# Experts 1 to 6 sorted by token count on the chip and computed at six widths, and the underflow mask replaced by a flag

## The chip, the cores and the metric

The kernel runs on one core of a Trainium2 chip. TensorE (PE) multiplies, VectorE (DVE), ScalarE (ACT) and GpSimd (POOL) do elementwise work, and SyncE (SP) and the others issue transfers. Each engine has its own queue of instructions. The metric is the device time of one launch in microseconds (us), as the median of several runs; less is better.

## The reference

Attention with pooled queries gives x, 1152 tokens of 512 values. Each token chooses two of eight experts; expert e takes its own tokens through two matrices with a ReLU between. A last dense block multiplies by w_in, applies h*cos(h) and multiplies by w_out. These two matrices, 512x2048 and 2048x512, come as 64-bit floats.

```python
top2 = np.argpartition(-noisy_logits, 2, axis=1)[:, :2]
...
for e in range(E):
    for k in range(2):
        mask = top2[:, k] == e
        h = np.maximum(x[mask] @ w1[e], 0.0)
        out[mask] += top2_w[mask, k, None] * (h @ w2[e])
...
h = x @ w_in
g = h * np.cos(h)
return (g @ w_out).astype(np.float32)
```

With the drawn inputs the experts 0 to 7 get 293, 306, 271, 255, 298, 284, 290 and 307 tokens.

## The kernel before

The program is written out in the order in which each engine runs it; a wait is put in wherever an instruction needs another engine's or a transfer's result. It has three parts: attention (to about 290 us of the profile), the experts (304 to about 575), the dense block (from there to the end).

**Routing.** `route` finds for every token its two experts and a row of the DRAM buffer `xg_d` for each. `scatter` writes the tokens there: 18 indirect transfers, issued by POOL one after another, each behind a tiny memset of `SPACER`. Expert 0 does not wait for them: its input is gathered on PE (`hot`). Expert 1 is loaded back from `xg_d` by POOL (`x_load(1)`, L961), later experts by SP.

**Experts.** Every expert has CAP = 320 slots for tokens, used or not. The loop runs over e and f, eight steps f for each expert, with s = 8e + f. In a step PE does `h_mm` (L975: 12 matmuls with 320 moving columns, since 32-bit values are split in a high and a low part and three products are made), ACT writes the high part `hh` (L985), DVE the low part `hl` (L986), and one step later PE does `yt_mm` (L1006: 12 more matmuls of 320 columns, 8 with `hh`, then 4 with `hl`) into four accumulators. So an expert has 8 x 24 = 192 matmuls. The next expert's tokens are loaded (`x_load`, tile `xr`), transposed on PE in four groups (`x_tr`, L967) and split by ACT and DVE (`x_split`, L913, L914). For expert 1 this stands at the end of expert 0 (f = 7): two groups of transposes, `yt_mm(0, 7)`, two more groups.

**Weights.** A unit is half a megabyte of w1 or w2. SP loads it into one of three `raw` buffers, ACT (L558) and DVE (L559) split it into `u`; `advance_c` runs this some units ahead of PE. All these stand in one queue for each engine with the steps' other work.

**Decode.** DVE turns 64-bit weights into 32-bit ones in 16 chunks during the experts: `dec_load` (two transfers of 512 KB by SP), then `dec` in three steps, DVE L1055, L1059, L1063. Values too small for 32 bits must become zero: ACT takes the absolute value (L1061), POOL makes a 0/1 mask (L1062) and multiplies (L1065) before it stores the chunk (L1066).

**Overflow.** `counts_of` (end of step s = 2) counts tokens per expert with one matmul and two DVE reductions; at the very end each engine loads the largest count, and a general path runs if it is over 320.

## Time and profile before

| | us |
|---|---|
| median of 3 runs | 793.23 (790.15 to 795.38) |
| the profiled execution | 794.18 |
| its span, first to last instruction | 792.3 |
| PE busy in it | 762.4 (96%) |
| DVE, ACT, POOL busy | 616.8, 508.2, 396.0 |

The span leaves about 2 us of the execution's own time outside. Busy time of PE includes pipelined waiting, so idle gaps and the granted clock have to be read from the timeline.

### The profile page before, as it was taken

The numbers are of one execution on the slowest core, as the hardware profiler recorded it, in microseconds if no ns is written. First come the engines' busy times: TensorE is split into PE (matmuls) and PEld (weight loads), VectorE is DVE, ScalarE is ACT, GpSimd is POOL, SyncE is SP. The second block draws the span as 40 slices with busy tenths as digits, with TensorE's granted clock in tenths as the row PEclk, the third lists the DMA queues.
The fourth block names the chain that finished last, engine by engine and source line by source line (L and its number), as shares of the span: only waits on it lengthen the run. The fifth ranks groups of instructions, "written<-read, shape, count | busy, mean of one in ns | idle before, by whom it ended". The sixth has DMA issues, their size and how long they took to land.

```text
span 792.3 us, 14073 instructions
## 1 busy us (share of the span) xinstructions
PE 762.4 (96%) x4976; PEld 703.7 (89%) x4976; DVE 616.8 (78%) x1226; ACT 508.2 (64%) x1218; POOL 396.0 (50%) x364
## 2 busy tenths in 40 slices
PE   7799999999999999799999999999999999999996
PEld 4689989999999989799999999999888999889995
DVE  5478778877888897379999999878678687785663
ACT  5689789879979854355654545555467566565553
POOL 4868767867878848316556666575056120100000
PEclk9899999999999999989999999999998999999999
DMA  9829688796964206967979979796633210100001
GB/s 211 174 61 208 149 206 205 209 251 148 244 154 146 61 18 213 333 204 235 331 254 317 306 268 348 245 334 212 221 102 118 80 31 25 54 1 27 2 1 43
DMA packets 91164, 133.67 MB, mean 169 GB/s; under 512 B 27952, under 2 KB 58032, under 8 KB 91088
## 3 DMA queue, kind: packets, MB, share of 16 engines
q1 hardware_dynamic: 84688, 111.21, 49.7%
q0 software_dynamic: 5392, 18.48, 6.5%
q10 hardware_dynamic: 1008, 3.02, 1.5%
q8 instruction: 41, 0.67, 0.3%
q14 instruction: 35, 0.29, 0.1%
HBM read 81.24 MB, written 29.88 MB: 140 GB/s over the span
## 4 chain that ended last, share of the span: by engine, by line
PE 72%; DVE 11%; DMA 5%; ACT 4%; POOL 3%; issue 3%; SPq 1%; ACTq 0%; DVEq 0%; POOLq 0%
PE h L975 17%; PE acc L975 12%; PE acc L1006 9%; PE s L282 9%; PE pa L360 8%; PE pt L322 7%; PE t L975 3%; DMA kt<-st 3%; DVE u L559 1%; PE t L967 1%; PE t L1022 1%; POOL xg_d L525 1%; PE pt L608 1%; DMA xr<-xg_d 1%; ACT cr L1327 1%
## 5 line engine op out<-in xcount | busy, mean ns | idle before, releaser
L298 DVE TENSOR_REDUCE nm<-s 128x1 f32<-128x384 f32 x216 | 108.0, 550 | 35.8 <-PE s L282 21.6
L307 ACT ACTIVATE p<-s,nm 128x384 f32<-128x384 f32 x216 | 126.2, 593 | 1.4 <-DVE nm L300 0.5
L975 PE MATMUL h<-xe,u 128*128 128x320 f32 x768 | 125.9, 313 | 0.0
L975 PEld LDWEIGHTS h<-xe,u 128*128 128x128 f32 x768 | 114.1, 188 | 2.2
L1062 POOL TENSOR_SCALAR raw<-raw 128x1024 f32<-128x1024 f32 x16 | 65.7, 4107 | 95.0 <-ACT raw L1061 90.7
L559 DVE TENSOR_TENSOR u<-raw,u 128x1024 fp32r<-128x1024 f32 x66 | 88.9, 1351 | 18.9 <-ACT u L558 18.7
L322 PE MATMUL pt<-ident,p 128*128 128x128 f32 x645 | 95.1, 275 | 0.2 <-DVE X L633 0.2
L282 PE MATMUL s<-kt,q 128*128 128x384 f32 x240 | 84.2, 372 | 7.8 <-DMA kt<-st 4.1
L335 ACT ACTIVATE eh<-pt 128x384 fp32r<-128x384 f32 x144 | 63.1, 491 | 39.3 <-PE pt L322 37.3
L360 PE MATMUL pa<-eh,v 128*128 128x320 f32 (+1 forms) x279 | 87.1, 326 | 0.0
L360 PE MATMUL pa<-el,v 128*128 128x320 f32 (+1 forms) x279 | 82.9, 311 | 0.0
L322 PEld LDWEIGHTS pt<-ident,p 128*128 128x128 f32 x645 | 77.6, 142 | 5.5 <-issue 1.9
L558 ACT ACTIVATE u<-raw 128x1024 fp32r<-128x1024 f32 x73 | 76.6, 1054 | 7.6 <-DMA raw<-w_d 4.6
L339 DVE TENSOR_TENSOR el<-pt,eh 128x384 fp32r<-128x384 f32 x144 | 73.2, 549 | 4.0 <-ACT eh L335 2.3
L1006 PE MATMUL acc<-hh,u 128*128 128x320 f32 x448 | 76.3, 313 | 0.0
L346 POOL TENSOR_TENSOR el<-rw,eh 128x384 fp32r<-128x384 f32 x71 | 71.7, 1010 | 5.9
L1006 PEld LDWEIGHTS acc<-hh,u 128*128 128x128 f32 x448 | 68.5, 190 | 0.1
L975 PE MATMUL acc<-u,gh 128*128 128x512 f32 x216 | 68.2, 397 | 0.0
...
L345 POOL TENSOR_SCALAR eh<-rw 128x384 fp32r<-128x384 f32 x71 | 36.6, 515 | 53.3 <-ACT rw L343 45.5
L282 PEld LDWEIGHTS s<-kt,q 128*128 128x128 f32 x240 | 44.8, 192 | 16.4 <-ACT p L307 7.7
L282 PE MATMUL s<-kt,l 128*128 128x384 f32 x168 | 56.6, 337 | 0.0
...
## 6 DMA issues: line engine op xcount, KB each, us to landing
raw<-in_moe_w_dram SPq DMA_DIRECT2D x64, 512.0 KB, 5.9
raw<-in_moe_w_in_dram SPq DMA_DIRECT2D x16, 512.0 KB, 4.5
raw<-in_moe_w_out_dram SPq DMA_DIRECT2D x16, 512.0 KB, 6.7
w_d<-dw POOLq DMA_DIRECT2D x16, 512.0 KB, 6.5
raw<-w_d SPq DMA_DIRECT2D x14, 512.0 KB, 4.2
xg_d<-ZERO SPq DMA_DIRECT2D x10, 512.0 KB, 5.1
...
```

What stands on the lines that cost most here:

```text
L282: nc.tensor.matmul(o, l, r, start=(m == 0), stop=(not lo and m == len(mm) - 1))
L298: nc.vector.tensor_reduce(NM[n][:, i:i + 1], SB[n][i][:, 0:384], axis=AX.X, op=OP.max, negate=True)
L307: nc.scalar.activation(P[n][i], SB[n][i][:, 0:384], AF.Exp, bias=NM[n][:, 3:4], accum_out=SUMS[:, t, 2 * hp + hl, i:i + 1])
L322: nc.tensor.transpose(p[:, c], P[n][j][:, c], ident)
L339: nc.vector.tensor_tensor(el, t_src(n, j), ef, op=OP.subtract)
L346: nc.gpsimd.tensor_tensor(el, rw, ef, op=OP.subtract)
L360: nc.tensor.matmul(st["p"][:, 0:w], V2[hp, hl, b][:, c, :], (EH, EL)[s][:, c, EB[g]:EB[g] + w], start=(c == 0 and s == 0), stop=(c == 8 an ...
L558: nc.scalar.activation(b[:, 0], r, AF.Copy)
L559: st_w["lo"].tensor_tensor(b[:, 1], r, b.bitcast(F32)[:, 0], op=OP.subtract)
L975: nc.tensor.matmul(o, l, r, start=first and i == 0, stop=last and i == len(seq) - 1)
L1006: nc.tensor.matmul(ACC[e, d][:, 0:CAP], w[:, i, 128 * d:128 * d + 128], r, start=f == 0 and r is hh and i == 0, stop=f == 7 and r is hl)
L1062: nc.gpsimd.tensor_scalar(m, m, 2.0 ** -15, 0.0, op0=OP.is_ge, op1=OP.add)
```

## The change

CAPS gives a width to each place in the loop: 320 for place 0 and 7, which keep experts 0 and 7, and 282, 288, 294, 302, 312, 320 for places 1 to 6. `counts_of` moves from the end of step 2 to the end of step 0. It now multiplies the counts by 8, adds the expert's number, sorts the eight numbers with one DVE `max` and takes the low three bits as the experts' ids (`RANKI`); it also fills a small tile of limits, `LIM`, which lies in the tile `U0`, by nine memsets on POOL. At the end of step 1 `load_ids` loads six ids into registers of SP and one into a register of POOL. Loads of weights and tokens and stores of results for places 1 to 6 take their address from these registers.

The mask of the decode is gone from POOL. ACT instead sums up, chunk by chunk, how far values lie under the limit (`FL`); in the last block (`small_weights`, i = 52) one matmul spreads the flag, and the general path, which now applies the mask itself, runs if a flag or a limit was passed. The first chunk's decode starts one step later (s = 9), the first two `dec_load` move from steps 5 and 6 to 7 and 9, and `yt_mm(0, 7)` now stands ahead of all four groups of `x_tr(1, ...)`.

```diff
     make_identity(nc, ident)
     XROWS = NT * 8 * 128
     CAP = 320
+    CAPS = (CAP, 282, 288, 294, 302, 312, CAP, CAP)
+    TOP = float(N)
     xg_d = dram.tile([XROWS, DM], F32, name="xg_d")
     y_d = dram.tile([XROWS, DM], F32, name="y_d")
     FF2 = w_in.shape[1]
...
                 if next(g, 0) == 0:
                     gens.remove(g)
 
+    def small_weights():
+        m = CNT8[:, 1:2]
+        nc.vector.tensor_reduce(m, FL, axis=AX.X, op=OP.max)
+        nc.vector.tensor_scalar(FLB, m.to_broadcast([128, 2]), 0.0, None, op0=OP.is_gt)
+        p = tb2()
+        nc.tensor.matmul(p[:, 0:2], ONES, FLB, start=True, stop=True)
+        nc.vector.tensor_scalar(m, p[:, 0:1], TOP, TOP, op0=OP.mult, op1=OP.min)
+        nc.vector.tensor_tensor(CNT, CNT8[:, 0:1], m, op=OP.max)
+
     def mix_weights():
         nc.vector.tensor_scalar(ROWC, ROW, 3071, None, op0=OP.min)
         d = WT[:, :, 1]
...
         nc.vector.reciprocal(w, w)
         nc.vector.tensor_tensor(d, w, d, op=OP.mult)
 
+    LIM = U0.rearrange("p t e -> p (t e)")[:, 0:10]
+
     def counts_of(bank):
         p = bank()
+        for i in range(8):
+            nc.gpsimd.memset(LIM[:, i:i + 1], 8.0 * CAPS[6 - i] + 7.0 if i < 6 else 8.0 * E_N * N)
+        nc.gpsimd.memset(LIM[:, 8:10], 8.0 * CAP + 7.0)
         nc.tensor.matmul(p[:, 0:8 * NT], ONES, MK.rearrange("p t e -> p (t e)"), start=True, stop=True)
         nc.vector.tensor_reduce(CNT8, p[:, 0:8 * NT].rearrange("p (t e) -> p e t", e=8), axis=AX.X, op=OP.add)
-        nc.vector.tensor_reduce(CNT, CNT8, axis=AX.X, op=OP.max)
+        nc.vector.scalar_tensor_tensor(CNT8, CNT8, 8.0, IOTA8, op0=OP.mult, op1=OP.add)
+        nc.vector.tensor_tensor(LIM[:, 8:10], CNT8[:, 0:8:7], LIM[:, 8:10], op=OP.subtract)
+        nc.vector.memset(CNT8[:, 0:8:7], 0.0)
+        nc.vector.max(RANK, CNT8)
+        nc.vector.tensor_copy(RANKI, RANK)
+        nc.vector.tensor_scalar(RANKI, RANKI, 7, None, op0=OP.bitwise_and)
+
+    def over_of():
+        nc.vector.tensor_tensor(LIM[:, 0:8], RANK, LIM[:, 0:8], op=OP.subtract)
+        nc.vector.tensor_reduce(CNT8[:, 0:1], LIM, axis=AX.X, op=OP.max)
+        nc.vector.tensor_scalar(CNT8[:, 0:1], CNT8[:, 0:1], 0.0, TOP, op0=OP.max, op1=OP.min)
+
+    EID = {0: (0, 0), 7: (7, 7)}
+
+    def load_ids():
+        def one(c, eng):
+            return nc.values_load(RANKI[0:1, c:c + 1], engines=[eng], min_val=0, max_val=E_N - 1)
+        for i in range(1, 7):
+            EID[i] = [one(6 - i, mybir.EngineType.SP), None]
+        EID[1][1] = one(5, mybir.EngineType.Pool)
+
+    def rows_of(e, which, st, n):
+        r = EID[e][which]
+        if e in (0, 7):
+            return slice(st * 1024 + e * 128, st * 1024 + e * 128 + n)
+        return bass.ds(r * 128 + st * 1024, n)
+
+    ysts = []
+
+    def y_store(eng, e, st, n, src):
+        eng.nop()
+        d = eng.dma_start(y_d[rows_of(e, 0, st, n)], src)
+        for o in ysts:
+            tc.declare_no_dep(d.ins, o.ins, reason="each expert and each block has rows of its own")
+        ysts.append(d)
 
     scat = []
 
...
         if u < NCONV:
             e, i = divmod(u, 8)
             if i % 2 == 0:
-                src = w1[e].rearrange("(a p) f -> p a f", p=128)[:, :, 128 * i:128 * i + 256]
+                we = w1[e:e + 1] if e in (0, 7) else w1[bass.ds(EID[e][0], 1)]
+                src = we.rearrange("o (a p) f -> p (o a) f", p=128)[:, :, 128 * i:128 * i + 256]
                 nc.sync.dma_start(r.rearrange("p (a f) -> p a f", a=4), src)
             else:
-                src = w2[e].rearrange("(a p) d -> p a d", p=128)[:, i - 1:i + 1, :]
+                we = w2[e:e + 1] if e in (0, 7) else w2[bass.ds(EID[e][0], 1)]
+                src = we.rearrange("o (a p) d -> p (o a) d", p=128)[:, i - 1:i + 1, :]
                 nc.sync.dma_start(r.rearrange("p (a d) -> p a d", a=2), src)
         else:
             st_w["eng"].dma_start(r, w32_d[u - NCONV])
```

```diff
-        mm3(o[:, 0:CAP], [(w[:, 0, kd, c], w[:, 1, kd, c], xh[:, kd], xl[:, kd]) for kd in range(4)], True, True)
+        n = CAPS[e]
+        mm3(o[:, 0:n], [(w[:, 0, kd, c], w[:, 1, kd, c], xh[:, kd, 0:n], xl[:, kd, 0:n]) for kd in range(4)], True, True)
         late = e == E_N - 1 and f >= 4
         hh, hl = ((hxs[0] if late else me).tile([128, CAP], F32R, name=f"h{i}", bufs=4) for i in "hl")
-        nc.scalar.activation(hh, o[:, 0:CAP], AF.Relu)
-        nc.vector.scalar_tensor_tensor(hl, o[:, 0:CAP], 0.0, hh.bitcast(F32), op0=OP.max, op1=OP.subtract)
+        nc.scalar.activation(hh[:, 0:n], o[:, 0:n], AF.Relu)
+        nc.vector.scalar_tensor_tensor(hl[:, 0:n], o[:, 0:n], 0.0, hh.bitcast(F32)[:, 0:n], op0=OP.max, op1=OP.subtract)
         HH[e, f] = (hh, hl)
...
         if i == 1:
             nc.vector.scalar_tensor_tensor(w, hi, -0x40000000, w, op0=OP.bitwise_and, op1=OP.bitwise_or)
         elif i == 2:
+            nc.vector.scalar_tensor_tensor(w, lo, 29, w, op0=OP.logical_shift_right, op1=OP.bitwise_or)
+            nc.gpsimd.dma_start(w32_d[f], w.bitcast(F32))
             nc.scalar.activation(m, m, AF.Abs)
-            nc.gpsimd.tensor_scalar(m, m, 2.0 ** -15, 0.0, op0=OP.is_ge, op1=OP.add)
-            nc.vector.scalar_tensor_tensor(w, lo, 29, w, op0=OP.logical_shift_right, op1=OP.bitwise_or)
-            wf = w.bitcast(F32)
-            nc.gpsimd.tensor_tensor(wf, wf, m, op=OP.mult)
-            nc.gpsimd.dma_start(w32_d[f], wf)
+            nc.scalar.activation(m, m, AF.Relu, scale=-1.0, bias=SMALL[:, 0:1], accum_out=FL[:, f:f + 1])
         if f < 2 and i == CD:
             conv(NCONV + f, DW[f].bitcast(F32))
 
...
     for i in range(NF2):
-        s0 = 8 + DQ * i // 15
+        s0 = 8 + DQ * i // 15 + (i == 0)
         for j in (0, 1, 2, CD):
             DECS.setdefault(s0 + j, []).append(lambda i=i, j=j: dec(i, j))
         if i + 2 < NF2:
             DECS.setdefault(s0 + 3, []).append(lambda i=i: dec_load(i + 2))
     for i in range(2):
-        DECS.setdefault(5 + i, []).append(lambda i=i: dec_load(i))
+        DECS.setdefault(7 + 2 * i, []).append(lambda i=i: dec_load(i))
     for d in range(4):
         ACC[0, d] = a_bank()
     for e in range(E_N):
...
             if not last and e and 3 <= f < 7:
                 x_tr(e + 1, f - 3)
             elif not e and f == 7:
-                x_tr(1, 0)
-                x_tr(1, 1)
                 yt_mm(0, 7)
-                x_tr(1, 2)
-                x_tr(1, 3)
+                for kd in range(4):
+                    x_tr(1, kd)
                 yt_evac(0)
             if s < NCONV - 1:
                 advance_c((5, 5, 6, 7, 8, 9, 11)[s] if s < 7 else s + LA + (s > 58))
...
+            if s == 0:
+                counts_of(tb2)
+            if s == 1:
+                load_ids()
             if s == 2:
                 mix_weights()
-                counts_of(tb2)
+                over_of()
             if not last:
                 if (e, f) in ((0, 1), (1, 0)):
                     x_load(e + 1)
...
+        if i == 3 * NF2 + 4:
+            small_weights()
         if 0 < i <= len(steps):
             g_split(*steps[i - 1])
```

The same widths stand in `x_split`, `x_tr`, `yt_mm`, `yt_evac` and the stores; the general path's loop over chunks is left out here.

**DVE, steps 0 to 2 of expert 0, before.** `hl` is the low part of a step, `u` a converted unit.

```order
L986 SCALAR_TENSOR_TENSOR hl<-h,hh 128x320 [waits Activation_49,Pool_49]
L559 TENSOR_TENSOR u_4740<-raw,u_4740 128x1024 [waits DMAHW2_49,Activation_49]
L559 TENSOR_TENSOR u_4741<-raw,u_4741 128x1024 [waits DMAHW3_49,Activation_49]
L986 SCALAR_TENSOR_TENSOR hl<-h,hh 128x320 [waits Activation_49] x2
L559 TENSOR_TENSOR u_4742<-raw,u_4742 128x1024 [waits DMAHW4_49,Activation_49]
L504 TENSOR_SCALAR ROWC<-ROW 128x18 [waits DVE_49]
```

In the changed kernel (its lines have other numbers; `U` is the tile of `LIM`):

```order
L1046 SCALAR_TENSOR_TENSOR hl<-h,hh 128x320 [waits Activation_49,Pool_49]
L617 TENSOR_TENSOR u_4746<-raw,u_4746 128x1024 [waits DMAHW2_49,Activation_49]
L617 TENSOR_TENSOR u_4747<-raw,u_4747 128x1024 [waits DMAHW3_49,Activation_49]
L538 TENSOR_REDUCE CNT_119<-t 128x8 [waits PE_49]
L539 SCALAR_TENSOR_TENSOR CNT_119<-CNT_119,IOTA_95 128x8 [waits DVE_49]
L540 TENSOR_TENSOR U_109<-CNT_119,U_109 128x2 [waits DVE_49,Pool_49]
L541 MEMSET CNT_119 128x2 [waits DVE_49]
L542 MAX RANK<-CNT_119 128x8 [waits DVE_49]
L543 CAST RANKI<-RANK 128x8 [waits DVE_49]
L544 TENSOR_SCALAR RANKI<-RANKI 128x8 [waits DVE_49]
L1046 SCALAR_TENSOR_TENSOR hl<-h,hh 128x320 [waits Activation_49] x2
```

The counting and sorting, L538 to L544, now stand ahead of the `hl` of steps 1 and 2, and the third of them waits for POOL.

**POOL, the last two scatters and what follows, before.**

```order
L525 DMA xg_d<-X,ROW 9216x512 [waits DMASW0_49]
L524 MEMSET SPACER 1x1 [waits Pool_49]
L525 DMA xg_d<-X,ROW 9216x512 [waits DMASW1_49]
L961 DMA xr<-xg_d 128x512 [waits DMASW1_49,DMASW2_49,PE_49,Activation_49]
L961 DMA xr<-xg_d 128x512 [waits DMASW3_49,PE_49]
L961 DMA xr<-xg_d 64x512 [waits DMASW4_49]
```

In the changed kernel:

```order
L580 MEMSET SPACER 1x1 [waits Pool_49]
L581 DMA xg_d<-X,ROW 9216x512 [waits DMASW1_49]
L535 MEMSET U_109 128x1 x8
L536 MEMSET U_109 128x2
L555 TENSOR_LOAD RANKI [waits DVE_49]
L555 ISA x2
L1020 ISA
L1020 DMA xr<-xg_d 128x512 [waits DMASW1_49,DMASW2_49,PE_49,Activation_49]
L1020 ISA
```

The memsets of `LIM` stand behind all 18 scatters, and the load of expert 1's tokens stands behind a register load.

**SP, the first weight loads after attention, before.** The first two are units 6 and 7, the third is unit 8, the first of expert 1.

```order
L549 DMA raw<-in_moe_w_dram 128x4x256 [waits DMAHW2_49,DMAHW1_49,DVE_49]
L552 DMA raw<-in_moe_w_dram 128x2x512 [waits DMAHW3_49,DVE_49]
L549 DMA raw<-in_moe_w_dram 128x4x256 [waits DMAHW4_49,DVE_49]
L552 DMA raw<-in_moe_w_dram 128x2x512 [waits DMAHW1_49,DVE_49]
L549 DMA raw<-in_moe_w_dram 128x4x256 [waits DMAHW5_49,DMAHW2_49,DVE_49]
```

In the changed kernel:

```order
L606 DMA raw<-in_moe_w_dram 128x4x256 [waits DMAHW2_49,DMAHW1_49,DVE_49]
L610 DMA raw<-in_moe_w_dram 128x2x512 [waits DMAHW3_49,DVE_49]
L555 TENSOR_LOAD RANKI [waits DVE_49]
L555 ISA x2
L555 TENSOR_LOAD RANKI
```

Behind units 6 and 7 SP now waits for the sorted ids and does six such register loads, and only then comes unit 8.

## Rows read from the trace of the kernel before

**Rows 1.** Busy time by stage (us busy, instructions), whole engines, one stretch of the experts.

```profile
371.00:405.00 34.00, 33.33 (x222) 31.33 (x221) 33.97 (x37) 18.47 (x29) 19.16 (x10) 1.00 0.85 279
```

**Rows 2.** Timeline of POOL: start us, us, line, operation.

```profile
322.18 0.97 POOL L525 DMA_INDIRECT xg_d<-X,ROW  x1 [0.21 <-issue]
328.50 1.70 POOL L961 DMA_DIRECT2D xr<-xg_d  x3 [5.35 <-DMA xg_d<-X,ROW]
```

**Rows 3.** Groups of POOL instructions, 296 to 542: line, count, busy us, mean ns, idle before.

```profile
L525 POOL DMA_INDIRECT xg_d<-X,ROW x18 | 19.9, 1106 | 12.6 <-DVE ROW L492 9.1 <-issue 3.3 <-DVE u L559 0.2
...
L524 POOL MEMSET SPACER<- 1x1 f32 x17 | 1.8, 105 | 0.0
```

**Rows 4.** Timeline of DVE around the first steps of expert 0.

```profile
307.32 2.36 DVE L559 TENSOR_TENSOR u<-raw,u 128x1024 fp32r<-128x1024 f32 x2 [0.39 <-ACT u L558]
309.60 0.48 DVE L986 SCALAR_TENSOR_TENSOR hl<-h,hh 128x320 fp32r<-128x320 f32 x1
...
315.01 0.23 DVE L516 TENSOR_REDUCE CNT<-t 128x8 f32<-128x72 f32 x1
```

**Rows 5.** Timeline of PE, expert 0 to the start of expert 1.

```profile
312.15 0.74 PE L1006 MATMUL acc<-hl,u 128*128 128x320 f32 x4
...
329.83 0.75 PE L1006 MATMUL acc<-hl,u 128*128 128x320 f32 x4
334.60 0.33 PE L967 MATMUL t<-ident,xr 128*128 128x128 f32 x1 [4.01 <-DMA xr<-xg_d]
...
340.49 1.84 PE L967 MATMUL t<-ident,xr 128*128 128x128 f32 x6
342.26 3.79 PE L975 MATMUL h<-xe,u 128*128 128x320 f32 x24
```

**Rows 6.** PE by stretch: busy us, instructions, granted clock, DMA share, GB/s.

```profile
330.00:334.00 4.00, 0.58 (x4) 1.00 1.03 300
...
336.00:340.00 4.00, 4.00 (x15) 0.50 0.88 314
...
342.00:343.00 1.00, 1.00 (x7) 0.85 0.00 0
```

**Rows 7.** Chain that ended last, merged: start us, us, operation; 320 columns, then 256.

```profile
406.30 1.76 PE h L975 x12
...
633.27 1.43 PE t L975 x12
```

**Rows 8.** Timeline of DVE: steps of the decode (L1055, L1059, L1063).

```profile
348.25 0.69 DVE L1055 TENSOR_SCALAR dw<-raw 128x1024 int32<-128x1024 int32 x1
...
351.87 1.22 DVE L1059 SCALAR_TENSOR_TENSOR dw<-raw,dw 128x1024 int32<-128x1024 int32 x1
...
354.54 2.12 DVE L1063 SCALAR_TENSOR_TENSOR dw<-raw,dw 128x1024 int32<-128x1024 int32 x1
...
359.26 2.94 DVE L1055 TENSOR_SCALAR dw<-raw 128x1024 int32<-128x1024 int32 x1
```

**Rows 9.** Who PE waited for, 342 to 575: us in total, times, longest.

```profile
PE t L1022 <- DVE yt L1016: 1.1, 2, 0.7
```

**Rows 10.** Groups of ACT instructions, 342 to 541.

```profile
L1061 ACT ACTIVATE raw<-raw 128x1024 f32<-128x1024 f32 x15 | 17.3, 1151 | 3.9 <-issue 3.1 <-DVE dw L1059 0.7
```

**Rows 11.** DMA issues: operation, count, KB each, median us to landing.

```profile
raw<-in_moe_w_dram SPq DMA_DIRECT2D x64, 512.0 KB, 5.9
...
raw<-in_moe_w_out_dram SPq DMA_DIRECT2D x16, 512.0 KB, 6.7
```

**Rows 12.** Timeline of SP at the end of the program.

```profile
784.97 1.70 SPq L1351 DMA_DIRECT2D out_dram<-os  x3
```

**Rows 13.** Timeline of DVE in a step of the last block.

```profile
774.85 0.56 DVE L1298 SCALAR_TENSOR_TENSOR cr<-cn,cr 128x384 f32<-128x384 f32 x1
```

**Rows 14.** Timeline of PE at the same place.

```profile
775.13 2.27 PE L975 MATMUL h<-x,u 128*128 128x384 f32 x12
```

**Rows 15.** Timeline of PE in the first block.

```profile
594.83 1.10 PE L1095 MATMUL t<-ident,cm 128*128 128x128 f32 x4 [1.95 <-DVE cm L1089]
```

More of the change, by code (lines that the diff above doesn't have):

```diff
@@ L965, in x_tr @@
         p = tb2()
-        for st, (s0, n) in enumerate(SW):
+        for st, (s0, n) in enumerate(SW[e]):
             nc.tensor.transpose(p[:, s0:s0 + n], XR[e, st][0:n, kd * 128:(kd + 1) * 128], ident[0:n, 0:n])
@@ L1005, in yt_mm @@
             for d in range(4):
-                nc.tensor.matmul(ACC[e, d][:, 0:CAP], w[:, i, 128 * d:128 * d + 128], r,
+                nc.tensor.matmul(ACC[e, d][:, 0:CAPS[e]], w[:, i, 128 * d:128 * d + 128], r[:, 0:CAPS[e]],
                                  start=f == 0 and r is hh and i == 0, stop=f == 7 and r is hl)
@@ L1027, in yt_out @@
             nc.scalar.activation(t[0:n], p[0:n], AF.Copy)
[L1028 to L1029 removed]
+        y_store(nc.sync, e, st, n, t[0:n])
     YT = {}
@@ L1405, in overflow @@
             nc.sync.dma_start(wm, w32_d.rearrange("f p c -> p f c"))
+            for f in range(NF2):
+                rm = ov.tile([128, 1024, 2], I32, name="orm")
+                nc.sync.dma_start(rm[:, 0:512].rearrange("p (a f) s -> p a (f s)", a=4),
+                                  w_in.bitcast(I32).rearrange("(a p) f -> p a f", p=128)[:, :, 256 * f:256 * f + 256])
+                nc.sync.dma_start(rm[:, 512:1024].rearrange("p f s -> p (f s)"), w_out.bitcast(I32)[128 * f:128 * f + 128])
+                m = rm.bitcast(F32)[:, :, 1]
+                nc.scalar.activation(m, m, AF.Abs)
+                nc.vector.tensor_scalar(m, m, 2.0 ** -15, None, op0=OP.is_ge)
+                nc.vector.tensor_tensor(wm[:, f], wm[:, f], m, op=OP.mult)
             with tc.For_i(0, E_N, 1) as e:
@@ L1469, in attn_moe_cos_kernel @@
     counts = nc.values_load(CNT[0:1, 0:1], min_val=0, max_val=N)
-    with tc.If(counts > CAP):
+    with tc.If(counts > 0):
         overflow()
```

41 lines of the change are left out of this document (23 added, 18 removed).

## The prediction

> **What bounds the kernel now.** I read the busy time by stage first: between 371 and 405 us PE is busy for 33.33 of 34 us, and DVE for 33.97 [rows 1]. So in the experts PE sets the pace, and DVE has nearly no room. Then I read the end of expert 0 in the timelines, because most of the moved instructions land there. PE finishes the step before last at about 330.5, waits 4.01 us for expert 1's tokens, and begins expert 1 at 342.26 [rows 5]. In the stretches the granted clock goes to 0.50 after that wait, which is 1.2 instead of 2.4 GHz, and is back by 343 [rows 6]. The reason for the wait stands in POOL's timeline: the last of 18 scatters starts at 322.18, and the load of the tokens can start only when the scatters have landed, at 328.50 [rows 2]. Last I read the chain that ended last: a group of 12 matmuls of 320 columns takes 1.76 us, one of 256 columns 1.43 us [rows 7].
>
> **Term 1, the widths.** The two kinds of group differ by 0.33 us for 12 x 64 columns, so a column costs 0.43 ns. The six places lose 38, 32, 26, 18, 8 and 0 columns, 122 in all, in 192 matmuls each: 122 x 192 x 0.43 ns = 10.1 us less on PE, which is on the path all through the experts. All widths lie between those of the two rows, so nothing has to be extrapolated. The Trainium skill (TensorE: Matmul & The Clock Gate, section "Wait — 56ns, not 53.3ns?") gives N / 2.4 GHz and about 2.5 ns for a matmul at full clock; as an estimate that would make 0.417 ns a column and 9.8 us, and the rows' 1.76 us for 12 lie above its 1.63.
>
> **Term 2, the counting ahead of `hl`.** The new DVE queue has the counting ahead of the low parts of steps 1 and 2, and its third instruction waits for POOL's nine memsets, which stand behind all scatters. POOL is not through with these before 322.18 + 0.97 = 323.15 [rows 2]; nine memsets at 0.105 us [rows 3] make it 324.1. DVE has done its two conversions by 309.7 [rows 4], does the reduction (0.23 us, in the same group) and one small operation more, and stands for some 14 us. Behind it then come four or five small dependent operations, some 0.2 us each by the nearest row, and the `hl` of step 1, 0.48 us [rows 4]: ready at 325.6. PE reaches the four matmuls that need it at 312.15, as before [rows 5], since the `hh` part does not wait. So PE stands idle from 312.3 to 325.6, about 13.3 us.
>
> That is not all lost, because PE would have waited for the tokens later. What PE still has to do then for expert 0 is the four `hl` matmuls and 11 groups of 12: 0.6 + 11 x 1.76 = 19.9 us, to 345.5. A wait brings the low clock again: after the 4.01 us it was at 0.50 from before 336 until past 342 [rows 6], some 6.4 us, half of which is lost. I take the same 3.2 us here (2 to 4), so 348.7. The tokens, which landed from 334.6 on [rows 5], are long there, even if POOL's register load costs a few us. Twelve transposes remain, now all behind `yt_mm(0, 7)`: six took 1.84 us at half clock [rows 5], so twelve at full clock 1.84, and about 1 us for two groups that wait for a free bank and the split of the one before: 2.9 us (1.8 to 3.9). Expert 1 starts at about 351.6 instead of 342.26: **9.3 us later** (7.5 to 11). That the old wait is gone is inside this number.
>
> That DVE cannot run past its waiting instruction rests on its queue being served in order. The Trainium skill (the same page, section "Architectural detail: the array is 16× 32×32, not 1× 128×128") says so of ACT, DVE and POOL; no row of this trace shows DVE held by POOL's queue in this place. If it were not so, the first rival below would be the forecast.
>
> **Term 3, the decode off POOL.** L1055 takes 0.69 us once and 2.94 another time, L1063 2.12 where the like L1059 takes 1.22 [rows 8]; the long ones run while POOL does its mask operations. Without these I count 0.69 + 2 x 1.22 = 3.1 us for a chunk instead of about 6.3, 3 us of DVE in every three steps. DVE's relief is worth only what PE waited for DVE: 1.1 us in the experts [rows 9]. I take **-1.1** (-2 to 0). ACT gets one more pass over each chunk, priced at the 1.15 us of its absolute value [rows 10], 18 us in all; ACT is busy for 18.47 of 34 us [rows 1], and the pass stands behind `hh` in its step, so I cost it at nothing. Were ACT full, it would delay `hh` by up to 1.15 us in 16 steps.
>
> **Term 4, what moved next to the start of expert 1.** `dec_load` of chunk 0 now comes two steps (7 us) ahead of the DVE instruction that needs it, and in SP's queue behind two weight loads that wait for DVE. A load of 512 KB takes 5.9 to 6.7 us to land [rows 11], so DVE stands for about 2 us with an `hl` behind it; chunks 1 and 2 likewise are nearer. PE has about a step of slack. I take **+1.5** (0 to 5; the upper end is one load's landing without that slack).
>
> **Term 5, the flag.** In step 52 PE's queue has the flag's matmul between two groups. DVE is through with that step's last arithmetic at 774.85 + 0.56 = 775.4 in a like step, PE with its group when the next starts, at 775.13 [rows 13, 14]. Two small DVE operations and the hand-over make it wait until about 775.8: **+0.6** (0.3 to 1). The wait is too short to be like the one behind which the clock fell.
>
> **The rest** I cost at nothing: register addresses add an instruction to each of SP's transfers, and SP issues only one or two in a step; narrower third transposes and stores shorten work that is hidden or tiny.
>
> **The sum** against the profiled execution: 9.3 - 10.1 - 1.1 + 1.5 + 0.6 = +0.2, so 794.4 for its 794.18. Against the median of 793.23 I forecast **793.4**: the 10 us that the widths give back are spent at the start of the experts.
>
> **The rivals.**
>
> *No stall.* If DVE is not held (or the scatters are issued much sooner), PE reaches the end of expert 0 as before, and `yt_mm(0, 7)` fills part of the old wait. Before, it ran behind that wait at the low clock, at twice its 1.76 us, so expert 1 starts 3.5 us earlier, at about 338.8, and term 2 turns from +9.3 to -3.5: 780.6. For it: nothing in the rows; against it: the order of the two queues. 10 in 100.
>
> *Slow register loads on SP (slower).* Six loads, one after another, stand ahead of unit 8 and start when the ids are ready, about 325.2. No row of before shows the price of one. A ceiling: at the end of the program SP loads the count after its last transfer is issued at 784.97 + 1.70 = 786.67 [rows 12], and the span ends at 792.3, so 5.6 us, with that transfer's landing in it. Lower end zero. Unit 8 is converted on ACT ahead of `hh(0, 6)`, which PE needs at about 345. With the load's 5.9 us [rows 11] SP must be free at about 337, so it decides at 2 us a load. At 3.6 us, six take 21.6, unit 8 lands at 352.7, PE waits some 9 us more, and the clock falls again (3.2): 793.4 + 12 = 805.5. I take 1 us a load, because the 5.6 us hold a landing and the whole end of the program as well. 10 in 100.
>
> *The widths do not count.* If a matmul were bound by its weight load, term 1 would be zero: 803.5. The 256-column groups have the same weight loads and take 1.43 us, so 2 in 100. The general path would cost far more, but the drawn counts of experts 1 to 6, 255, 271, 284, 290, 298 and 306, fit the six widths.
>
> *The stall in the first block moves.* DVE holds PE for 1.95 us at 594.83 [rows 15], and the low clock follows. If work shifts against POOL's there, 5 us go: 788. 8 in 100; the same could come up where there is none now.
>
> **How the numbers follow.** The forecast has 70 in 100. Its own range, from the bounds of the terms, is 789 to 800. With the first-block stall and parts of the two main rivals 8 in 10 lie between **784 and 801**. Differences within 1% (7.9 us) can hardly be told from no change here. Faster by over 1%: no stall, 10, and favourable ends together, 6: 0.16. Slower: slow loads, 10, the widths, 2, and unfavourable ends, 2: 0.14. The same: 0.70.
>
> **What would show it.** In the new profile: DVE idle from about 310 to 324 in front of the subtraction from `LIM`, released by POOL; PE idle from 312 to 325.6, then some 6 us at clock 0.50; no wait of PE for `xr` at the end of expert 0; expert 1 beginning near 351.6; groups of 12 at 1.76 - 12 x 38 x 0.43 ns = 1.56 us in place 1, 1.62 in place 3; L1055 at 0.7 us throughout. I would be wrong if PE's idle time there were under 8 us, if ACT waited for unit 8, or if PE waited for DMA or DVE in places 1 to 6 for more than 3 us.

## The result, and the profile after

The changed kernel takes **802.1 us** (801.67 to 803.32, 4 runs), the kernel before 793.78 (790.15 to 795.38, 4 runs): a ratio of 1.0111, 95% interval 1.0075 to 1.0147. It is slower by 1.1%. The profiled execution has 803.32 us and a span of 801.6.

To see where the time went I took the start of the same TensorE instruction in both timelines:

| place | before | after | after minus before |
|---|---|---|---|
| attention, ahead of the first fill of `y_d` | 187.47 | 186.66 | -0.8 |
| end of the routing | 300.04 | 306.53 | +6.5 |
| first `h` of expert 1 | 342.26 | 354.53 | +12.3 |
| a step of place 1 | 372.05 | 387.52 | +15.5 |
| transposes of place 6's output | 542.08 | 547.71 | +5.6 |
| expert 7 | 556.40 | 562.84 | +6.4 |
| last block, ahead of the flag | 731.29 | 737.23 | +5.9 |
| last block, behind it | 739.66 | 748.08 | +8.4 |
| span | 792.3 | 801.6 | +9.3 |

The first loss, 7.3 us, lies in a stage for which the prediction has no term. Windows there, of before and then of after (us, then busy us and instructions of PE, PEld, DVE, ACT, POOL, then granted clock, DMA share, GB/s):

```profile
208.00:212.00 4.00, 4.00 (x32) 3.95 (x31) 2.93 (x8) 3.06 (x10) 3.39 (x5) 1.00 0.95 228
212.00:216.00 4.00, 4.00 (x30) 3.82 (x30) 3.46 (x10) 3.99 (x13) 3.33 (x5) 1.00 0.93 251
```

```profile
208.00:212.00 4.00, 3.81 (x28) 3.50 (x26) 2.51 (x6) 2.21 (x8) 3.35 (x5) 1.00 0.87 183
212.00:216.00 4.00, 0.00 (x0) 0.00 (x0) 0.00 (x0) 0.00 (x0) 1.40 (x1) 0.78 0.79 184
216.00:220.00 4.00, 2.65 (x12) 2.61 (x12) 1.40 (x3) 3.19 (x10) 0.35 (x1) 0.50 0.64 178
```

PE, DVE and ACT stand still together, and the DMA engines, 0.93 busy before, are at 0.79 and move 184 GB/s instead of 251. Behind the stand PE's granted clock is 0.50, its lower level, in 216 to 220. What PE waits for, and what that waits for, in the timelines of PE, ACT and SP of after:

```profile
217.35 0.90 PE L324 MATMUL pt<-ident,p 128*128 128x128 f32 x3 [5.54 <-ACT st L175]
```

```profile
216.81 0.49 ACT L175 ACTIVATE st<-pt 128x384 f32<-128x384 f32 x1 [6.60 <-DMA kt<-st]
```

```profile
199.35 1.70 SPq L433 DMA_DIRECT2D y_d<-ZERO  x1
...
205.38 2.25 SPq L244 DMA_DIRECT2D kt<-st  x1
```

ACT may write `st` again only when the transfers that read it have landed. They stand in SP's queue behind the fill of `y_d`, which the change makes 102 partitions high instead of 64 (L433). This part of the change the diff ahead of the prediction leaves out:

```diff
-            d, o = (xg_d, 0) if i < 10 else (y_d, 64)
+            d, o, w = (xg_d, 0, 64) if i < 10 else (y_d, min(CAPS) - 256, 384 - min(CAPS))
...
-            nc.sync.dma_start(dst, ZERO[0:64, None, :].to_broadcast([64, 4, DM]))
+            nc.sync.dma_start(dst, ZERO[0:w, None, :].to_broadcast([w, 4, DM]))
```

In the same stretch the median from issue to landing of `kt<-st` goes from 5.2 us to 9.1, by these groups of DMA issues of before and of after:

```profile
kt<-st SPq DMA_DIRECT2D x2, 288.0 KB, 5.2
```

```profile
kt<-st SPq DMA_DIRECT2D x2, 288.0 KB, 9.1
```

Next the stall of term 2. In after, the places that answer to [rows 2], [rows 4], [rows 5] and [rows 6]: POOL, then ACT's `hh` of step 1, DVE, PE, and PE's windows.

```profile
327.65 0.97 POOL L581 DMA_INDIRECT xg_d<-X,ROW  x1 [0.22 <-issue]
328.62 0.32 POOL L535 MEMSET U<- 128x1 f32 x8
```

```profile
314.63 0.43 ACT L1045 ACTIVATE hh<-h 128x320 fp32r<-128x320 f32 x1
```

```profile
329.01 0.16 DVE L540 TENSOR_TENSOR U<-CNT,U 128x2 f32<-128x2 f32 x1 [12.49 <-POOL U L536]
...
329.82 0.88 DVE L1046 SCALAR_TENSOR_TENSOR hl<-h,hh 128x320 fp32r<-128x320 f32 x2
```

```profile
330.37 1.44 PE L1066 MATMUL acc<-hl,u 128*128 128x320 f32 x4 [11.42 <-DVE hl L1046]
...
353.45 1.14 PE L1026 MATMUL t<-ident,xr 128*128 128x128 f32 x6 [0.45 <-DVE xe L973]
354.53 3.39 PE L1034 MATMUL h<-xe,u 128*128 128x282 f32 x24
```

```profile
323.00:324.00 1.00, 0.00 (x0) 0.00 (x0) 0.00 (x0) 0.00 (x0) 0.78 (x3) 0.74 0.75 303
324.00:330.00 6.00, 0.00 (x0) 0.00 (x0) 0.82 (x6) 0.00 (x0) 4.31 (x16) 0.50 0.59 224
330.00:334.00 4.00, 3.63 (x14) 3.64 (x15) 2.96 (x11) 0.21 (x1) 1.71 (x3) 0.53 0.17 57
334.00:338.00 4.00, 4.00 (x30) 4.00 (x29) 1.72 (x2) 1.38 (x2) 0.00 (x0) 1.00 0.72 218
```

The queue stands as forecast: DVE waits 12.49 us for POOL's memsets, which run behind the last scatter, and does the `hl` of step 1 only behind them, though its `hh` was there by 315.1. PE waits 11.42 us for `hl`, and there is no wait for expert 1's tokens any more. The clock fell at about 323.5, while PE still stood, and is back by 334, so PE works at the lower level only from 330.37 on, for 3.4 us. In the kernel before, the clock fell when PE had resumed (334.60 in [rows 5]), and PE worked through the whole of the low stretch, to 342.3 by [rows 6]. A window of before:

```profile
335.00:336.00 1.00, 0.41 (x2) 0.23 (x2) 0.00 (x0) 0.00 (x0) 0.00 (x0) 0.74 1.01 332
```

Then the decode, in the timelines of DVE and PE, and the same stretch as [rows 1]:

```profile
367.86 0.69 DVE L1114 TENSOR_SCALAR dw<-raw 128x1024 int32<-128x1024 int32 x1 [3.16 <-DMA raw<-in_moe_w_out_dram]
```

```profile
368.97 0.79 PE L1066 MATMUL acc<-hl,u 128*128 128x282 f32 x4 [2.44 <-DVE hl L1046]
370.88 0.30 PE L1026 MATMUL t<-ident,xr 128*128 128x128 f32 x1 [1.12 <-DMA xr<-xg_d]
```

```profile
371.00:405.00 34.00, 32.49 (x225) 30.27 (x225) 27.30 (x39) 23.71 (x37) 1.88 (x4) 0.95 0.93 319
```

Behind its late start the decode is as fast as forecast, POOL is nearly empty (1.88 us of 34), and DVE has 7 us of room in 34 where it had none. The steps that answer to [rows 8], and a group of 12 in place 1 from the chain of waits, which answers to [rows 7]:

```profile
384.33 1.22 DVE L1120 SCALAR_TENSOR_TENSOR dw<-raw,dw 128x1024 int32<-128x1024 int32 x1
...
400.22 0.69 DVE L1114 TENSOR_SCALAR dw<-raw 128x1024 int32<-128x1024 int32 x1
```

```profile
386.64 1.56 PE acc L1066 x12
```

Last the flag, in the timelines of DVE and PE:

```profile
740.81 0.56 DVE L1357 SCALAR_TENSOR_TENSOR cr<-cn,cr 128x384 f32<-128x384 f32 x1
741.28 0.16 DVE L513 TENSOR_REDUCE CNT<-FL 128x1 f32<-128x16 f32 x1
741.48 0.17 DVE L514 TENSOR_SCALAR FLB<-CNT 128x2 bf16<-128x2 f32 x1
```

```profile
741.70 0.16 PE L516 MATMUL t<-FLB,ONES 128*128 128x2 bf16 x1 [2.22 <-DVE FLB L514]
```

The two flag operations stand behind the cosines of the next step in DVE's queue (L1357), so PE waits 2.22 us, not the 0.6 of term 5.

### The profile page after: what moved, and what is told of

Read it like the earlier page. It is cut to its first block, busy times and chain, and to the rows that moved or that the text cites. A ratio compares the mean times of both kernels' runs of the same rounds, so it can differ in the third digit from the quotient of the medians.

```text
span 801.6 us, 14183 instructions
## 1 busy us (share of the span) xinstructions
PE 754.4 (94%) x4977; PEld 697.2 (87%) x4977; DVE 580.3 (72%) x1238; ACT 526.5 (66%) x1250; POOL 284.3 (35%) x342
## 4 chain that ended last, share of the span: by engine, by line
PE 67%; DVE 8%; DMA 7%; ACT 7%; POOL 6%; issue 3%; SPq 1%; ACTq 0%; DVEq 0%; POOLq 0%
PE h L1034 18%; PE acc L1034 11%; PE acc L1066 10%; PE s L284 7%; PE pt L324 6%; PE pa L362 6%; DMA kt<-st 4%; PE t L1034 3%; POOL st L231 1%; PE t L1026 1%; ACT p L309 1%; POOL xg_d L581 1%; DMA xr<-xg_d 1%; PE s L287 1%; POOL el L348 1%
## 5 line engine op out<-in xcount | busy, mean ns | idle before, releaser
L1034 PE MATMUL h<-xe,u 128*128 128x320 f32 (+5 forms) x768 | 122.9, 310 | 0.0
L1034 PEld LDWEIGHTS h<-xe,u 128*128 128x128 f32 x768 | 111.8, 192 | 1.9
L617 DVE TENSOR_TENSOR u<-raw,u 128x1024 fp32r<-128x1024 f32 x66 | 80.5, 1223 | 30.4 <-ACT u L616 30.4
L284 PE MATMUL s<-kt,q 128*128 128x384 f32 x240 | 86.0, 379 | 3.4 <-DMA kt<-st 1.8
L1121 POOL DMA_DIRECT2D w_d<-dw x16 | 8.5, 534 | 208.3 <-DVE dw L1120 208.3
L1066 PE MATMUL acc<-hh,u 128*128 128x320 f32 (+5 forms) x448 | 71.7, 302 | 0.0
L1066 PEld LDWEIGHTS acc<-hh,u 128*128 128x128 f32 x448 | 64.8, 188 | 0.0
L284 PEld LDWEIGHTS s<-kt,q 128*128 128x128 f32 x240 | 45.4, 195 | 13.3 <-ACT p L309 7.9
L1034 PE MATMUL h<-x,u 128*128 128x256 f32 (+1 forms) x384 | 56.8, 297 | 0.0
```

Source lines behind the costliest of these rows:

```text
L284: nc.tensor.matmul(o, l, r, start=(m == 0), stop=(not lo and m == len(mm) - 1))
L617: st_w["lo"].tensor_tensor(b[:, 1], r, b.bitcast(F32)[:, 0], op=OP.subtract)
L1034: nc.tensor.matmul(o, l, r, start=first and i == 0, stop=last and i == len(seq) - 1)
L1066: nc.tensor.matmul(ACC[e, d][:, 0:CAPS[e]], w[:, i, 128 * d:128 * d + 128], r[:, 0:CAPS[e]], start=f == 0 and r is hh and i == 0, stop=f = ...
```

## The experiments

They ran on three chips: e1 to e4 and e9 to e12 on one, e5 to e8 on a second, e13 to e15 on a third. Beside them the kernel before had medians of 793.56 us (e1 to e4), 798.35 (e5 to e8), 794.81 (e9 to e12) and 798.75 (e13 to e15), so times are compared through the ratio to it, and the times that the expectations for e5 to e8 and e15 name can't be compared as they stand. A ratio of 0.004 is 3 us, which is as much as some of the edits are worth. So what is concluded rests first on this table: by how much TensorE fell behind (+) or gained (-) against the trace of before in five stretches (times of the trace before), worked out as in the table above.

| run | 187-300 fill | 300-346 expert 0 | 346-372 decode | 372-542 places 1 to 6 | 731-740 flag | ratio, 95% interval |
|---|---|---|---|---|---|---|
| after | +7.3 | +5.4 | +3.6 | -9.8 | +2.5 | 1.0111, 1.0075 to 1.0147 |
| e1 | +1.2 | +5.6 | +1.2 | -9.2 | +2.5 | 1.0071, 1.0024 to 1.0119 |
| e2 | +6.8 | +0.1 | +0.4 | 0.0 | 0.0 | 1.0124, 1.0095 to 1.0152 |
| e3 | +1.4 | -0.7 | +0.3 | +0.4 | 0.0 | 1.0015, 0.9984 to 1.0046 |
| e4 | +8.1 | -3.2 | +2.0 | -9.7 | +4.0 | 1.0017, 0.9988 to 1.0045 |
| e5 | +7.8 | +5.6 | -1.3 | -9.7 | +2.5 | 1.0020, 1.0002 to 1.0038 |
| e6 | +7.0 | +5.3 | +2.9 | -9.9 | +0.1 | 1.0033, 1.0008 to 1.0059 |
| e7 | +8.6 | +6.2 | +4.0 | -2.3 | +2.5 | 1.0213, 1.0170 to 1.0255 |
| e8 | -0.2 | +5.0 | -1.7 | -9.7 | +0.1 | 0.9895, 0.9860 to 0.9929 |
| e9 | +1.6 | -4.2 | -1.7 | -9.7 | +0.1 | 0.9834, 0.9789 to 0.9880 |
| e10 | +0.9 | -3.1 | +1.2 | -9.7 | +2.5 | 0.9921, 0.9893 to 0.9948 |
| e11 | +0.6 | -4.6 | -1.5 | -9.7 | +0.1 | 0.9838, 0.9799 to 0.9877 |
| e12 | +0.1 | -0.3 | 0.0 | +0.2 | 0.0 | 0.9979, 0.9947 to 1.0011 |
| e13 | +2.0 | +5.2 | +0.5 | 0.0 | 0.0 | 1.0014, 0.9982 to 1.0047 |
| e14 | +49.6 | +4.9 | 0.0 | +0.2 | 0.0 | 1.0615, 1.0549 to 1.0681 |
| e15 | +1.5 | +5.7 | -1.8 | -9.7 | +0.1 | 0.9919, 0.9884 to 0.9954 |

**The fill.** Five runs change nothing but the partitions of the two fills of `y_d`; e1 in the changed kernel, the others in the kernel before. The edit (e1; e2, e3, e13 and e14 have 102, 112, 104 and 103 in the kernel before, always up to partition 127):

```diff
-            d, o, w = (xg_d, 0, 64) if i < 10 else (y_d, min(CAPS) - 256, 384 - min(CAPS))
+            d, o, w = (xg_d, 0, 64) if i < 10 else (y_d, 16, 112)
```

e1. 

> The changed kernel with one edit: the two fills of y_d with zeros write 112 partitions (896 KB) instead of 102 (816 KB). In the changed kernel TensorE stands idle from 211.8 to 217.4 us in the attention, the clock falls, and 7.3 us are lost there, while the transfers around the second fill land in 8 to 10 us instead of 5 to 6. Theory A, the number of partitions: a transfer over 102 partitions is spread badly over the DMA engines and holds up what is queued behind it; 112 is a multiple of 16 like the 64 of before, so the wait goes and the time is 802.1 - 7.3 = 795 us (794 to 797). Theory B, the bytes: 816 KB instead of 512 KB are too many there; 896 KB are more still, so the wait stays or grows: 802 to 804. Theory C, something else in the change (not the fill): 802. The Trainium skill (DMA: Bandwidth & Descriptors, section on why a DMA increments its semaphore by 16 and not by 1) says that a transfer uses the largest number up to 16 that divides its slowest dimension; that is theory A, with 6 engines for 102 and 16 for 112.

Median 796.41 us. The wait at 212 us is gone; a window of e1 there:

```profile
212.00:216.00 4.00, 4.00 (x31) 3.95 (x32) 3.65 (x11) 4.00 (x13) 2.00 (x3) 1.00 0.95 311
```

It has more bytes than after, and the DMA engines are at 0.95 with 311 GB/s. Theory A holds in the trace (6.1 us back), where the ratio alone would not have settled it.

e2. 

> The kernel before with one part of the change: its two fills of y_d write 102 partitions from row 26 on, 816 KB each, instead of 64 partitions and 512 KB. Theories A (partitions) and B (bytes): the wait of TensorE near 212 us comes up here too, 793.8 + 7.3 = 801 us (798 to 803). Theory C (something else in the change): 793.8 us, no wait there.

Median 801.7 us: this edit alone makes the kernel before as slow as the changed kernel, 6.8 us of it in the attention. Theory C falls.

e3. 

> The kernel before with its two fills of y_d over 112 partitions, 896 KB each. Theory A (partitions): no wait in the attention, 793.8 to 795.5 us. Theory B (bytes): the wait comes up as with 102 partitions or is longer, 800 to 804 us. Theory C: 793.8 us.

Median 794.74 us: with the most bytes of all, 1.4 us are lost. Theory B falls.

e13. 

> The kernel before with its two fills of y_d over 104 partitions from row 24 on, 832 KB each. By the rule that a transfer uses as many DMA engines as the largest number up to 16 that divides its partitions, 104 gives 13 engines, where 102 gave 6 and 112 gave 16. Theory K (that rule sets the wait): little wait in the attention, 0.5 to 3 us, ratio to the kernel before 1.001 to 1.004. Rival K2 (any number that isn't a multiple of 16 does it, or what lies above some number of bytes per engine): the wait as with 102 partitions, 5 to 7 us, ratio 1.008 to 1.012.

Median 799.74 us beside 798.75: two partitions more than e2, and 2.0 us lost in the attention instead of 6.8. Rival K2 falls. (Its +5.2 in expert 0 is another matter, below.)

e14. 

> The kernel before with its two fills of y_d over 103 partitions, 824 KB each; no number but 1 divides 103 up to 16. Theory K: the fill runs on one engine, and what is queued behind it waits far longer than with 102: at the 240 GB/s that the trace shows for all 16 engines, one carries some 15 GB/s, so 824 KB take some 55 us; the loads behind it are held for tens of us if they need that engine, 820 to 860 us in all, at any rate above 810. Rival K2: as with 102, 799 to 803 us.

Median 848.76 us: with one partition more than e2 the attention loses 49.6 us instead of 6.8. A window of it, and its SP timeline behind the first of these fills and behind the second:

```profile
216.00:224.00 8.00, 0.00 (x0) 0.00 (x0) 0.00 (x0) 0.00 (x0) 0.00 (x0) 0.52 0.07 26
```

```profile
203.37 25.59 SPq L239 DMA_DIRECT2D kt<-sh  x1
...
237.34 28.90 SPq L418 DMA_DIRECT2D y_d<-ZERO  x1
```

The share of the DMA engines is 0.07, one in sixteen, at 26 GB/s, and SP itself is held for 25.59 and 28.90 us at the issue behind a fill. So 103 partitions run on one engine, at 26 GB/s and not the 15 that the expectation took. The losses stand in the order that theory K gives, 49.6, 6.8, 2.0 and 1.4 us for the divisors 1, 6, 13 and 16, while the bytes rise by less than a tenth. For the other numbers no view counts the engines, but the traces hold a record of every packet. The fill's packets are those of 2 KB, and most of their time is spent with this many of them under way at once: 1 with 103 partitions (90% of the packets' time in e14), 6 with 102 (60% in after, 61% in e2); with 104 and 112 the number that has the largest share is 13 (30% in e13, 35% in e15) and 16 (29% in e3, 32% in e1). These are theory K's numbers. All these fills end at partition 127, so the row where they begin changes with their number; no run varies it alone. The Trainium skill (DMA: Bandwidth & Descriptors, section "Why a DMA increments its semaphore by 16 and not by 1") states the rule: the largest number up to 16 that divides the slowest dimension on both sides of the transfer. The runs agree with it, and where the page has no price they have one.

**The stall.** e4 writes the limits at the start of the program, into a tile that is free till then:

```diff
+    LIM = FL[:, 0:10]
+    for i in range(8):
+        nc.gpsimd.memset(LIM[:, i:i + 1], 8.0 * CAPS[6 - i] + 7.0 if i < 6 else 8.0 * E_N * N)
+    nc.gpsimd.memset(LIM[:, 8:10], 8.0 * CAP + 7.0)
...
-        for i in range(8):
-            nc.gpsimd.memset(LIM[:, i:i + 1], 8.0 * CAPS[6 - i] + 7.0 if i < 6 else 8.0 * E_N * N)
-        nc.gpsimd.memset(LIM[:, 8:10], 8.0 * CAP + 7.0)
```

e4. 

> The changed kernel with one edit: the nine GpSimd memsets of the limits write a part of the tile FL at the start of the program, so that VectorE's counting no longer waits for what stands behind the scatters in GpSimd's queue. Theory S (that wait is what holds hl of step 1): VectorE isn't idle from 316 to 329 us, TensorE doesn't stand at 319 to 330 us, the step before last of expert 0 runs on before the tokens of expert 1 land, and expert 1 starts about 9 us sooner, 802.1 - 9.3 = 793 us (791 to 796). Rival S2 (the tokens then set the end, since they land no sooner, and the whole of the wait comes back with the low clock): 797 to 799 us. Rival S3 (VectorE waits there for something else): 802 us.

Median 794.4 us, ratio 1.0017 against 1.0111: 0.0094, 7.5 us. In the stretch of expert 0 it goes from +5.4 to -3.2, which is 8.6 us; theory S holds, and S2 and S3 fall. PE's timeline in e4:

```profile
339.89 1.44 PE L1065 MATMUL acc<-hh,u 128*128 128x320 f32 x8 [1.58 <-ACT hh L1044]
343.32 0.77 PE L1025 MATMUL t<-ident,xr 26*128 26x26 f32 x4 [0.82 <-DMA xr<-xg_d]
```

The 11.42 us are gone, and of the old wait for tokens only 0.82 is left, because the step `yt_mm(0, 7)` now runs ahead of the transposes.

**Decode, flag and widths**, each alone in the changed kernel:

```diff
-        DECS.setdefault(7 + 2 * i, []).append(lambda i=i: dec_load(i))
+        DECS.setdefault(5 + i, []).append(lambda i=i: dec_load(i))
```

e5. 

> The changed kernel with one edit: the first two decode loads go back to steps 5 and 6 (in the changed kernel 7 and 9). In the trace of the changed kernel VectorE waits 3.16 us for the first chunk at 367.86, TensorE 2.44 us for hl behind it and 1.4 us more for tokens, the clock falls, and some 4 us are lost from expert 1 to expert 2. Theory D (the late load is the cause): these waits go, 802.1 - 4 = 798 us. Rival D2 (the load's landing is slowed by what else is in the queue there, and moving it only moves the wait to the weights or tokens): 801 to 803 us.

Median 799.89 us. The stretch 346 to 372 goes from +3.6 to -1.3, so 4.9 us come back, and PE has no wait for `hl` left there: theory D. But the late load doesn't always cost as much. Other kernels that keep it are at +1.2 (e1, e10) to +4.0 (e7). In e10, PE's wait for this `hl` is shorter than the 2.44 us of after:

```profile
351.28 0.79 PE L1065 MATMUL acc<-hl,u 128*128 128x282 f32 x4 [0.91 <-DVE hl L1045]
```

From e10 to e9, on one chip, the stretch goes from +1.2 to -1.7, so 2.9 us come back there.

```diff
-        nc.vector.tensor_reduce(m, FL, axis=AX.X, op=OP.max)
-        nc.vector.tensor_scalar(FLB, m.to_broadcast([128, 2]), 0.0, None, op0=OP.is_gt)
...
+        if i == 3 * NF2 + 3:
+            flag_pre()
```

(`flag_pre` holds the two lines taken out of `small_weights`.)

e6. 

> The changed kernel with one edit: the two VectorE operations that make the flag stand one step earlier, ahead of that step's cosines; the matmul of the flag and what follows it stay. In the trace of the changed kernel TensorE waits 2.22 us at 741.70 for the flag, since VectorE's next-step cosines stand ahead of it. Theory G: the wait goes, 802.1 - 2.3 = 799.8 us, and no wait of TensorE for VectorE near 742. Rival G2 (TensorE then waits for a bank of PSUM behind the flag's read instead): 801 to 802 us.

Median 801.29 us. The stretch of the flag goes from +2.5 to +0.1, and the flag's matmul in PE's timeline of e6 has no wait ahead of it: theory G.

```profile
739.18 0.18 PE L519 MATMUL t<-FLB,ONES 128*128 128x2 bf16 x1
```

```diff
-        w = CAPS[e]
+        w = CAP
...
-    SW = [[(0, 128), (128, 128), (256, c - 256)] for c in CAPS]
+    SW = [[(0, 128), (128, 128), (256, c - 256)] for c in [CAP] * 8]
```

(and so in `h_mm`, `yt_mm` and `yt_evac`.)

e7. 

> The changed kernel with all widths of the experts' arithmetic, loads and stores back at 320, and its fill of 102 partitions, sorting, flag and decode kept. Theory W (0.43 ns a column, 122 columns, 192 matmuls each): 802.1 + 10.1 = 812.2 us, up to 813 with the 0.5 us more that the shifts between the traces show. Rival W2 (widths don't count, what is gained comes from the decode off GpSimd): 802 to 804 us.

Median 814.65 us. Between 372 and 542 it gains 2.3 us against before where the changed kernel gains 9.8. These 7.5 us are the widths of places 2 to 6, for which the prediction's price gives 84 x 192 x 0.43 ns = 6.9; W2 falls. Place 1 lies ahead of 372, mixed with the decode. Over the whole, e7's profiled span is 810.4 - 801.6 = 8.8 us above that of after, and by the ratios (1.0213 and 1.0111) it loses 8.1 us more, where theory W has 10.1. The 2.3 us are the rest of the change in the experts at the old widths; I put them down to the decode off POOL, which no run undoes alone.

**All four mended.** e8 and e9 put the edits of e1, e4, e5 and e6 together. e10 has those of e1 and e4 alone, e11 all four with the counting, the register loads and the load of expert 1's tokens one step later, and e15 all four with 104 partitions.

e8. 

> The changed kernel with four edits together: fills of 112 partitions, limits written early, decode loads at steps 5 and 6, flag one step earlier. If the four losses are separate: 802.1 - 6 (fill, which keeps 1.3 us for its bytes) - 9.3 - 4 - 2.3 = 780.5 us (778 to 783). Rival (the tokens of expert 1 or the weights then set the end of expert 0, so that the limits and the decode give back only part): 785 to 789 us. If the losses were accidents of a single execution: 794 or more.

Median 789.59 us, ratio 0.9895. The losses of fill, decode and flag are gone; the expert 0 stretch is at +5.0, as if nothing had been done there. PE's timeline in e8:

```profile
314.36 0.73 PE L1068 MATMUL acc<-hl,u 128*128 128x320 f32 x2
315.36 0.63 PE L1068 MATMUL acc<-hl,u 128*128 128x320 f32 x1 [0.27 <-issue]
317.48 0.31 PE L1068 MATMUL acc<-hl,u 128*128 128x320 f32 x1 [1.49 <-issue]
318.88 0.31 PE L1036 MATMUL h<-xe,u 128*128 128x320 f32 x1 [1.09 <-issue]
...
322.39 2.83 PE L1036 MATMUL h<-xe,u 128*128 128x320 f32 x10 [1.66 <-issue]
```

The profile shows nothing that PE waits for: it runs one or two matmuls of a group and stands for up to 1.7 us in front of the next, and ACT and DVE stand too. This lasts to 322.4, some 2 us past the end of POOL's last scatter (320.2).

e9. 

> The kernel with all four edits once more. In its first trace TensorE, ScalarE, VectorE and SyncE stand in front of instructions that wait for nothing shown, from 309 to 322 us, in steps of some 1.3 us, while GpSimd issues its scatters; this costs about 8 us. Theory P (it belongs to this kernel's timing): the same gaps come again, ratio to the kernel before 0.99, 785 to 790 us. Theory Q (an accident of that execution or chip): no such gaps, expert 1 starts about 3.5 us sooner than in the kernel before instead of 5 us later, and the time is 779 to 782 us.

Median 783.0 us, ratio 0.9834, no such gaps on this chip: expert 0 is at -4.2. The time lies between the two theories' ranges, 1 us above that of Q; the trace decides, and theory P falls as a property of this kernel's timing.

e10. 

> The changed kernel with two edits only: limits written early and fills of 112 partitions; decode loads and flag stay late. Theory P: if the gaps of the kernel with four edits come from the fill together with the early limits, they are here too: 780.5 + 4 + 2.3 + 8 = 795 us. Theory Q: no gaps, 802.1 - 6 - 9.3 = 787 us (785 to 789).

Median 788.63 us; no gaps, as theory Q has it, and the losses of decode and flag are still there (+1.2 and +2.5).

e11. 

> The kernel with all four edits, and the counting and the six register loads of SyncE one step (3.5 us) later. In the first trace of the four edits the gaps begin where VectorE has the ids ready (309.0 us) and SyncE begins its register loads. Theory R (these loads next to the scatters make the gaps): they begin 3.5 us later here, and end where the scatters end, so about 2 us less is lost: 785 us. Theory P without R: gaps at the same place as in the kernel with four edits, 787 us. Theory Q: no gaps, 780 us.

Median 782.16 us, ratio 0.9838, no gaps. Since e9 on the same chip has none either, it says nothing about theory R; it is no faster than e9. What speaks against R is e13 below: it has the gaps and no such register loads.

e12. 

> The kernel before, unchanged, for a second profile of it on the chip of this call. On the chip of the second call its median was 798.35 us instead of 793.6 on the first. If a chip changes only the attention, the shift stands ahead of 300 us in the trace; if it is the memory's pace, it is spread over the stages. 793 to 799 us.

Median 791.84 us; it shows only how far two traces of one kernel on that chip differ, 0.3 us at most in the five stretches. It doesn't answer the question on the second chip.

The third chip, where the kernel before also had about 798 us, says more. e13, which is the kernel before but for its fills, has the gaps there. PE's timeline in e13:

```profile
316.17 0.60 PE L975 MATMUL h<-xe,u 128*128 128x320 f32 x3 [0.82 <-issue]
317.60 0.30 PE L975 MATMUL h<-xe,u 128*128 128x320 f32 x1 [0.83 <-issue]
...
319.72 0.31 PE L975 MATMUL h<-xe,u 128*128 128x320 f32 x1 [0.85 <-issue]
```

e15. 

> The kernel with all four edits, its fills of y_d over 104 partitions instead of 112: 128 KB less in all. Theory K: 13 engines and fewer bytes give about the same, within 1.5 us of the 783.0 us (ratio 0.9834) of 112 partitions. Rival K2: the wait of 102 partitions comes back, 788 to 790 us, ratio 0.991.

Median 791.62 us, ratio 0.9919. The fill is at +1.5, so the wait isn't back; the expert 0 stretch has the gaps, +5.7 as in e8. Neither reading of the expectation fits its ratio, because it was written against a chip without gaps; beside e8 (0.9895), which had them too, 104 and 112 partitions don't differ measurably.

So the mended kernel is faster than the kernel before everywhere it ran: by 1.7% (1.2 to 2.1) where there are no gaps, and by 0.8 to 1.1% where there are. The changed kernel was slower by 1.1%.

## Why the prediction was wrong

The forecast was 793.4 us and no change; it is 802.1, above the upper end of the range, 801. Taken step by step:

- **The step that failed** is "The rest I cost at nothing". The change takes the two fills of `zero_fill` from 64 to 102 partitions, 512 to 816 KB each, and the prediction has no term for it at all, not even in the list of what it costs at nothing. It costs 7.3 us (e1 and e2: 6.1 and 6.8), nearly the whole of the result. It isn't hidden, since in SP's queue the fill stands ahead of transfers whose source ACT wants to write again, and those land 9.1 instead of 5.2 us after their issue. Going by the bytes would have misled too: 112 partitions, 896 KB, cost 1.4 us.
- **Term 2, the stall**, was right in its mechanism and too large: 12.27 - 6.49 = 5.8 us at the first `h` of expert 1, against 9.3 (7.5 to 11). PE's idle time is 11.42 instead of 13.3, because POOL is through 1 us sooner (328.62, less the 6.5 us of shift, is 322.1 against 323.15) and its eight memsets take 0.32 us together. And PE works at the low clock for 3.4 us, not 6.4, since the clock had fallen while PE still stood; that halves the 3.2 us set for it.
- **Term 1, the widths**, was right in its price: 1.56 us for a group of 12 in place 1, as worked out, and 7.5 us against 6.9 for places 2 to 6. Over the whole kernel e7 gives 8.1 to 8.8 us of the 10.1; place 1's share can't be told from the decode's waits there.
- **Term 3** was right in kind, 2.3 us against 1.1 (0 to 2). That the additional ACT pass costs nothing was not quite right. In after PE waits for ACT's `ys` in front of the output transposes three times, where before it waited for DVE's `yt`, and the row below, from the waits of PE in after, gives 1.9 us for it, against 1.1 for the wait of [rows 9]. No run undid that pass alone, so its share in the +0.8 us of expert 7 is argued only.

```profile
PE t L1083 <- ACT ys L1088: 1.9, 3, 1.0
```

- **Term 4** was mis-sized: 4.9 us (e5), or 2.9 from e10 to e9, against 1.5 (0 to 5). The wait of DVE is 3.16 us rather than 2, PE waits for 2.44 us of that and so has no step of slack, and behind its two waits the clock falls (0.95 in the mean from 371 to 405), which the term left out. With this a sign that the prediction named for being wrong came true: from 354 to 548 PE waits 4.0 us for DMA and DVE, over the 3.
- **Term 5** was mis-sized: 2.4 us (e6) against 0.6. I took the end of DVE's arithmetic from a step of its kind. But in the code of the step the cosines of the next unit stand ahead of the flag. The clock, which the term leaves out for a short wait, stayed up behind these 2.22 us in after. In e4 the flag's wait is 2.22 us too, but the clock falls behind it, and the stretch loses 4.0 us. A window of e4:

```profile
736.00:738.00 2.00, 2.00 (x7) 1.71 (x7) 0.43 (x2) 0.99 (x2) 0.00 (x0) 0.50 0.00 0
```

- **The rivals.** *No stall* didn't occur, but e4 shows that its price was right: -3.2 in that stretch where it said -3.5. *Slow register loads* did not occur: the ids are ready at 329.9, and SP issues the load of unit 8 at 333.87, so six loads took less than 4 us. That rival's 805.5 lies nearer to the result than the forecast does, for another reason. *The widths do not count* is excluded by e7. The stall of the first block stayed where it was: the wait for `cm` is 1.9 us in after and 1.95 in [rows 15].

The shifts between the traces add up: -0.8 + 7.3 + 5.8 for the start, 15.5 - 12.3 = 3.2 and then -9.8 for the experts, +0.8 in expert 7, -0.5 in the blocks, +2.5 for the flag, and 0.9 behind the flag, most of it between the last matmul and the end of the span: 9.4 for the 9.3 between the spans. What the last 0.9 is remains open. Outside the fill the terms' errors are -3.5 (stall), +3.4 (decode, by e5), +1.9 (flag) and smaller ones, and they nearly cancel: without the fill's 7.3 us the forecast would have been some 2 us off, and that is luck more than sizing.
